# The query normaliser of block 1 of each linear-attention layer spread through sixteen DRAM rows instead of indicator matmuls, with instruction order, engine choice and buffers searched anew

## The chip, the core and the metric

The kernel runs on one core of a Trainium2 chip. The core has five engines with a queue of their own: PE (TensorE, matmuls; PEld is its weight load), DVE (VectorE), ACT (ScalarE), POOL (GpSimd) and SP (SyncE), which here issues the DMAs. An engine takes its instructions in the order in which the program lists them; engines wait for one another through semaphores. The metric is device time in microseconds (us) of one execution, as the median of several runs. The profile comes from one further execution.

## What is computed

Four layers, A B A B, act on x of 2048 tokens by 512 features (bf16), each behind a layer norm and with a residual. There are 32 heads of 16 features. The change lies in layer A, a linear attention whose features are two softmaxes, of sign plus and minus:

```python
phi_q = concat([softmax(pq), softmax(-pq)], -1)      # per head, 32 features
phi_k = concat([softmax(pk), softmax(-pk)], -1)
kv  = einsum("bhsf,bhsd->bhfd", phi_k, v)
z   = einsum("bhsf->bhf", phi_k)
num = einsum("bhqf,bhfd->bhqd", phi_q, kv)
den = einsum("bhqf,bhf->bhq", phi_q, z)[..., None] + 1e-6
x   = x + (num / den) @ wo
```

Layer B is a local attention: each token sees 8 keys, two tokens apart.

## The kernel before, in words

The 2048 tokens are four blocks of 512 (b = 0 to 3); L is 0 or 1, the first or second pair of layers A and B. A weight fold at the start joins the query and key projections with `w_phi`, so that one matmul gives pq or pk. The stages carry the names of their functions and the digits L and b:

- `s_a1` (lines 582 on, stage a1_Lb): key projection `mk`, value projection `mv`, exponentials `ek` of both signs, the sums of 16 by a tree of additions on DVE (`t8` to `t1`), reciprocals as exp(-ln) on ACT (`rr`), the product `mul`, and the sums kv and z over all tokens in PSUM (`kv`).
- `s_a2` (688 on, a2_Lb): query projection `mq` into PSUM, four products of four matmuls per block; `eq` writes the exponentials of both signs to the tile `Eq`, eight ACT instructions per block; `ms` sums them per head by 32 small matmuls, `rs` takes the reciprocal `rS` (an Ln and an Exp on ACT).
- `s_akv` (730 on): once per L, when all four blocks have added to kv: copy of kv to SBUF (`ev`), transposes (`tr`), then the masked matrices `ZM` (`z`) and `R` (`r`) on DVE.
- `s_a3` (770 on, a3_Lb), the stage that the change touches: `md` gives the denominators by 32 small matmuls of `Eq` with `ZM`; `dr` (line 786, two DVE instructions), `ln` (794, Ln and Exp on ACT) and `rho` (798, DVE) give the normaliser rho, one number for each head, sign and token, in a tile of 128 partitions by 256. Each of these numbers must then multiply the 16 feature rows of its head in `Eq`. There are two ways to do this:
  - By indicator matmuls: `bc` (803) spreads one sign of rho over the feature rows with 16 matmuls of 32 by 128 into four PSUM banks; for each of the 4 banks of each of the two signs `bev` (841) either copies the bank to SBUF as bf16 on ACT (tile `bs`) or does nothing, and `mulp` (812) multiplies 128 by 512 of `Eq` on DVE, from `bs` or straight from PSUM.
  - Through DRAM: `wr` (819) writes rho to a scratch tensor `rd` of 16 rows by two DMAs of 64 KB, `rdb` (826) reads it back for one sign, each row for eight partitions, as a tile `Prho` of 512 KB, and `muld` (833) multiplies 128 by 2048 of `Eq` on DVE, two instructions per block.
- `s_a4` (885 on): `mo` applies `R` (32 small matmuls, reading all of `Eq`), `ev` copies to the tile oT, and `s_out` (508) does the output projection `mm`, the residual `res` (on DVE, or on ACT where PE adds x by a matmul with the identity), the squares for the layer norm `sq` (ACT), `var`, `ln`, `nmr`, the layer norm application `ap`, and the transposed copy of the result by DMA or on PE.
- `s_b1` (919 on): query, key and value projections of layer B (`mm`, line 927), values written to DRAM (`vwr`) and read back four times (`vrep`). `s_b2`: the products `prod` of queries with eight shifted keys (DVE, 128 by 4096), their sums on PE (`lgt`), exponentials and their normaliser `pt`. `s_b3`: products `pav` with the values (DVE, 128 by 4096), sums (`mo`) and the output projection.

Which blocks go through DRAM stands in `_OPT["rho_dma"]` (line 39). Nothing is scheduled at run time: `stages` lists the steps as threads, `run` issues them in the order of the string `_ORDER` (line 56), `_CHOICE` (99) says for each step that two engines can do which of them does it, and `_SLOTS` (107) gives every tile its buffer in the pools `big` (8), `med` (16), `t2` (6) and `ps` (8 PSUM banks). On each engine a step stands behind all that were issued to it earlier.

## Time and profile before

| what | value |
|---|---|
| median of 3 runs | 328.9 us (327.68 to 329.29) |
| the profiled execution's own time | 327.1 us |
| its span in the profile | 325.3 us |
| moved by DMA | 41.05 MB, mean 126 GB/s |
| DVE is last busy at | 320.55 us |

The 1.8 us between span and time lie around the profiled span. The profile gives, for each engine, the union of its busy intervals; matmuls overlap in their pipeline, so that a matmul's own duration is longer than the distance from one to the next. A row of the timeline has start, duration, engine, line, operation, tiles and count, and in brackets the idle time of the engine ahead of it with what ended it.

### The profile page before, as it was taken

The numbers are of one execution on the slowest core, as the hardware profiler recorded it, in microseconds if no ns is written. First come the engines' busy times: TensorE is split into PE (matmuls) and PEld (weight loads), VectorE is DVE, ScalarE is ACT, GpSimd is POOL, SyncE is SP. The second block draws the span as 40 slices with busy tenths as digits, with TensorE's granted clock in tenths as the row PEclk, the third lists the DMA queues.
The fourth block names the chain that finished last, engine by engine and source line by source line (L and its number), as shares of the span: only waits on it lengthen the run. The fifth ranks groups of instructions, "written<-read, shape, count | busy, mean of one in ns | idle before, by whom it ended". The sixth has DMA issues, their size and how long they took to land.

```text
span 325.3 us, 8025 instructions
## 1 busy us (share of the span) xinstructions
PE 309.9 (95%) x3174; PEld 150.0 (46%) x3174; DVE 299.5 (92%) x435; ACT 283.2 (87%) x641; POOL 21.6 (7%) x50
## 2 busy tenths in 40 slices
PE   8999999999999999989999999979999999999883
PEld 3654456445454444444444445644544454533331
DVE  5999996988999998999999899699999999999993
ACT  4999989998898899899998999999999998775570
POOL 4000000000001001000000000000023031500000
PEclk9999999999999999999999999999999999999998
DMA  7948100023535897692740300023533947728952
GB/s 201 344 105 209 52 2 4 2 59 90 115 98 131 166 233 230 214 221 45 222 134 1 66 1 2 4 56 93 148 68 121 229 116 185 213 103 246 248 181 91
DMA packets 43853, 41.05 MB, mean 126 GB/s; under 512 B 28448, under 2 KB 37664, under 8 KB 43808
## 3 DMA queue, kind: packets, MB, share of 16 engines
q1 hardware_dynamic: 43280, 40.45, 46.8%
q8 instruction: 26, 0.43, 0.5%
q14 instruction: 19, 0.16, 0.2%
q10 hardware_dynamic: 528, 0.02, 0.1%
HBM read 27.74 MB, written 6.95 MB: 107 GB/s over the span
## 4 chain that ended last, share of the span: by engine, by line
PE 38%; ACT 21%; DVE 20%; DMA 7%; issue 6%; SPq 5%; DVEq 0%; ACTq 0%
PE ps L927 15%; PE ps L519 8%; SPq L983 5%; ACT sqd L539 3%; DMA Vg<-vd 3%; DVE pav L1075 3%; DVE prod L1013 3%; DMA vd<-V 3%; ACT Eq L705 3%; PE ps L697 3%; DVE Ek L650 2%; PE ps L604 2%; DVE stat L492 2%; ACT xn L445 2%; ACT oT L191 2%
## 5 line engine op out<-in xcount | busy, mean ns | idle before, releaser
L927 PE MATMUL ps<-xnT,WB 128*128 128x512 bf16 x384 | 87.2, 380 | 0.1
L1075 DVE TENSOR_TENSOR pav<-PT,Vg 128x4096 bf16<-128x4096 bf16 (+1 forms) x34 | 72.2, 2164 | 1.7 <-DMA Vg<-vd 1.2
L1013 DVE TENSOR_TENSOR prod<-QT,K 128x4096 bf16<-128x4096 bf16 x32 | 71.8, 2284 | 0.3
L927 PEld LDWEIGHTS <-WB 128*128 128x128 bf16 x384 | 42.6, 114 | 42.2 <-issue 5.6
L519 PEld LDWEIGHTS <-oT 128*128 128x128 bf16 x256 | 24.1, 98 | 32.2 <-ACT oT L191 2.7
L705 ACT ACTIVATE Eq<-ps 128x512 bf16<-128x512 f32 x64 | 34.9, 615 | 0.3 <-PE ps L697 0.3
L191 ACT CAST oT<-ps 128x512 bf16<-128x512 f32 (+1 forms) x55 | 30.4, 588 | 5.5 <-PE ps L1084 5.1
L598 ACT ACTIVATE Ek<-ps 128x512 bf16<-128x512 f32 x64 | 34.0, 621 | 0.0
L519 PE MATMUL ps<-WoB,oT 128*128 128x512 bf16 x128 | 32.5, 380 | 0.9 <-ACT oT L191 0.9
L697 PE MATMUL ps<-xnT,WA 128*128 128x512 bf16 x128 | 31.6, 379 | 0.6 <-ACT bs L846 0.3
L539 ACT ACTIVATE sqd<-x 128x512 bf16<-128x512 bf16 x48 | 30.4, 632 | 1.8 <-DVE x L532 0.6
L604 PE MATMUL ps<-WA,xnT 128*128 128x512 bf16 x128 | 30.5, 379 | 0.1
L592 PE MATMUL ps<-WA,xnT 128*128 128x512 bf16 x128 | 30.5, 379 | 0.0
L519 PE MATMUL ps<-WoA,oT 128*128 128x512 bf16 x128 | 29.8, 380 | 0.1
L532 DVE SCALAR_TENSOR_TENSOR x<-ps,x 128x512 bf16<-128x512 f32 x35 | 22.9, 683 | 0.2 <-PE ps L519 0.2
L529 ACT ACTIVATE x<-ps 128x512 bf16<-128x512 f32 x29 | 16.8, 607 | 4.9 <-PE ps L522 4.9
L191 ACT CAST QT<-ps 128x512 bf16<-128x512 f32 x31 | 18.3, 600 | 3.0 <-PE ps L927 3.0
L1084 PE MATMUL ps<-pav,indAV 128*32 128x512 bf16 (+1 forms) x272 | 17.3, 369 | 2.9 <-DVE pav L1075 2.9
L604 PEld LDWEIGHTS <-xnT 128*128 128x128 bf16 x128 | 12.3, 98 | 15.6 <-issue 1.0
L445 ACT ACTIVATE xn<-x,nmr,rstd 128x512 bf16<-128x512 bf16 x23 | 18.1, 819 | 1.4 <-DVE nmr L434 1.3
L191 ACT CAST K<-ps 128x512 bf16<-128x512 f32 x31 | 17.9, 597 | 1.1 <-PE ps L927 1.0
L592 PEld LDWEIGHTS <-xnT 128*128 128x128 bf16 x128 | 12.2, 98 | 14.2 <-issue 0.2
(128 smaller groups left out, 434.9 us busy)
## 6 DMA issues: line engine op xcount, KB each, us to landing
Vg<-vd SPq DMA_DIRECT2D x128, 131.5 KB, 3.4
vd<-V SPq DMA_DIRECT2D x8, 528.0 KB, 3.3
Prho<-rd SPq DMA_DIRECT2D x8, 512.0 KB, 5.7
x<-in_A_x_dram SPq DMA_DIRECT2D x3, 512.0 KB, 7.5
WB<-in_B_wqkv_dram SPq DMA_DIRECT2D x3, 512.0 KB, 9.1
wraw<-in_A_wqkv_dram SPq DMA_DIRECT2D x4, 256.0 KB, 3.9
out_dram<-x SPq DMA_DIRECT2D x8, 128.0 KB, 2.4
out_dram<-x SPq DMA_DIRECT2D x4, 256.0 KB, 2.4
```

The source lines that it names most:

```text
L191: self.nc.scalar.copy(out=out, in_=in_)
L445: nc.scalar.activation(out=xn, in_=xt, func=ACT.Identity, scale=rstd, bias=sh)
L519: nc.tensor.matmul(y[:], lhsT=oT[:, c, t * P:(t + 1) * P], rhs=Wo()[:, c, :], start=(c == 0), stop=(c == NB - 1 and not onpe))
L539: nc.scalar.activation(out=sqd[:], in_=xb[:, t, :], func=ACT.Square, accum_out=T["ss"][:, t:t + 1])
L592: nc.tensor.matmul(pk[:], lhsT=xnT[:, t, k, :], rhs=self.WA[:, k, D:2 * D], start=(k == 0), stop=(k == NB - 1))
L598: nc.scalar.activation(out=T["E"][:, t, s, :], in_=T["k", t][:], func=ACT.Exp, scale=1.0 - 2.0 * s)
L604: nc.tensor.matmul(pv[:], lhsT=xnT[:, t, k, :], rhs=self.WA[:, k, 2 * D:3 * D], start=(k == 0), stop=(k == NB - 1))
L697: nc.tensor.matmul(pq[:], lhsT=self.WA[:, k, hb * P:(hb + 1) * P], rhs=xnT[:, :, k, :], start=(k == 0), stop=(k == NB - 1))
L705: nc.scalar.activation(out=self.Eq[L, b][s][:, :, hb, :], in_=T[hb][:].rearrange("p (t i) -> p t i", t=4), func=ACT.Exp, scale=1.0 - 2.0 * s)
L927: nc.tensor.matmul(pp[:], lhsT=self.WB[:, k, i * D + c:(i + 1) * D:NB], rhs=xnT[:, :, k, :], start=(k == 0), stop=(k == NB - 1))
L1013: nc.vector.tensor_tensor(out=pr[:], in0=QT[:, c:c + 1, :].to_broadcast([P, NW, TB]), in1=win, op=ALU.mult)
L1075: nc.vector.tensor_tensor(out=pv, in0=PT[:, :, lo:lo + n].unsqueeze(1).to_broadcast([P, NB, 2, n]), in1=vw, op=ALU.mult)
```

## The change

`rho_dma` gains the blocks (0, 1) and (1, 1), so that block 0 alone of each layer A keeps the indicator matmuls. `_ORDER`, `_CHOICE` and `_SLOTS` are replaced as wholes; no function is changed.

```diff
 _OPT = {
-    "rho_dma": ((0, 2), (0, 3), (1, 2), (1, 3)),
+    "rho_dma": ((0, 1), (0, 2), (0, 3), (1, 1), (1, 2), (1, 3)),
...
 _ORDER = """
-23 2 8 a d 0 9 b 0 4f j k i i i o j i i i i i 0 t 1m 1n i i l i p 2 1m 1o 0 t o u 3 i i i m n 1t 1u 1m 1p q t 1m
...
+8 4f 30 i 0 j i i i 9 k i i i i i i i 2 1m 0 0 a b i i 2 1m i j l m 0 3 o p t 1n o f t u 1o 1t 1u 1m 1p 3 n 1m
...
 _CHOICE = (
-    "1111110111000111111110000000100001001101000101010111101100001000001101010000100000000000111110111101"
...
+    "0111110011100111111110100000100001000110010100100011101111110100111111001000100001000000101100110101"
...
 _SLOTS = {
-        "0123456789abcdef153437ad3335063b941fced7a94c1f5c09a1f3bcaa45e09673210af7b3c45164425511f457186d32bc0a"
...
+        "0123456789abcdef24536399d4d9b79c831ef268314dfe68bbb714689c0e7182b3f9d2e6307fc1be2cb111901cea418d2b7f"
...
```

In instructions, PE loses 64 weight loads and 64 matmuls of `bc`, SP gains 4 writes and 4 reads, and DVE and ACT change in these kinds (count before, count after):

```
DVE  mulp from bs 128x512     14   3      ACT  bev 128x512          14   3
DVE  mulp from PSUM 128x512   18  13      ACT  copies of v to vaug  21  25
DVE  muld 128x2048             8  12      ACT  ap of the layer norm 23  26
DVE  copies of v to vaug      11   7
DVE  ap of the layer norm     41  38
```

Five further kinds of PSUM copies change by one or two instructions. The order around the kv sum of the second layer A, as the strings give it (digits are L and b, then the step's number; d: straight from PSUM, s: through `bs`):

```
PE  before: kv13(3), mq13(0), tr, ms12, md10, mq13(1), md12, bc10(0), bc10(1), md11, mq13(2), mq13(3), mo10
PE  after:  kv13(3), mq12(3), tr, md10, ms12, md11, md12, bc10(0), ms11, bc10(1), mq13(0) to mq13(3), mo10

ACT before: kv copy, 1 eq12, 2 eq13, rs12, ln10, 2 eq13, bev10, ln12, bev10 x3, eq13, bev10, eq13, ln11, 2 eq13, ...
ACT after:  kv copy, 5 eq12, ln10, rs12, bev10, ln12, rs11, bev10, ln11, 8 eq13, ev10, rs13, ln13, res10, ...

DVE before: z, r, dr10, rho10, dr12, mulp10 d s d, rho12, dr11, mulp10 s s d s s, rho11, ev10 x2, mulp11 d d s s, ...
DVE after:  z, r, dr10, rho10, dr12, rho12, mulp10 d, dr11, mulp10 d s, rho11, mulp10 d d s d d, ev10 x3, dr13, muld12 x2, ...

SP  before: wr12, rdb12 x2, wr13, rdb13 x2
SP  after:  wr12, wr11, rdb12 x2, rdb11 x2, wr13, rdb13 x2
```

From `mo10` to the first product of layer B, `prod10(0)`, ACT has 15 PSUM copies, 9 `sq` and 2 layer norm `ln` before, and 8 copies, 12 `sq` and 3 `ln` after, beside the same 3 `res`, 3 `ap`, one copy of 1024, `rs13` and `ln13`. From `prod10(0)` to the end DVE has 16 `prod`, 16 `pav` and 4 `pt` in both. On PE the projections of layer B that stand ahead of the step `mo13` are seven before (four of keys, two of queries, one of values) or seven after (three of queries and four of keys). In the first layer A, PE has `ms00`, two kv steps, `mq02(0)`, `tr`, `ms01`, `md00`, `md01`, `mq02(1)`, `bc00(0)` before, and `ms00`, `tr`, `md00`, `ms01`, `md01`, `mq03(0)`, `bc00(0)` after.

More of the change, by code (lines that the diff above doesn't have):

```diff
@@ new lines @@
+6x 6t 6v 4w 4z 50 6y 51 4z 50 4z 52 6v 50 53 4v 4z 50 54 81 81 86 88 88 6v 6z 88 9f 9i 84 9f 9j 9n 55 56 55 55
+9k 58 6v 55 6z 70 85 7q 87 7q 9p 73 71 72 74 9p 59 57 57 89 9w 9x 88 5a 57 89 57 5b 57 9w 89 89 8a 9p 9p bh 9q
+9o 9s 8a 9r 87 87 bs 87 89 5b 5f 5d 5e 5c aw 8a at bt bt bs bs 9t bt bt bt bt 9x 9w 9x ax 9w 5g 9x at at au 88
+8b 8b 8b au au au aw 9y ay 9y ai bq br br al am 9x 9y al 87 al 9e 9v 9v 9v aj aj an 8c 8d 8c 8c 8b 8c bq bq 8g
+bq ao 8f 8e 8h 8h at 8h au au br br 8i 8j ai au 9w br br br br au 9z a0 a1 9v 9v 9z a0 9z 9z 8k a0 bq a3 a0 a2
@@ L103 @@
-    "0000000001111011000000000000000000000000000000000010110000000000000000000001111"
+    "0111110011100111111110100000100001000110010100100011101111110100111111001000100001000000101100110101"
+    "0000110100000000000000001111101000100000100000000000000000001000111110000001000100000000000000000000"
+    "1111110000000000010000011011011111011100001010000100000000000111110010000111000000000000000001111010"
+    "000000001000000000000000000000000001110000000000000000000001111"
 )
```

90 lines of the change are left out of this document (41 added, 49 removed).

## Prediction

> **What bounds the kernel now.** First the page's engine shares, then the table of busy time by stage, which says where the shares are full.
>
> ```profile
> PE 309.9 (95%) x3174; PEld 150.0 (46%) x3174; DVE 299.5 (92%) x435; ACT 283.2 (87%) x641; POOL 21.6 (7%) x50
> ```
>
> ```profile
> 6.00:209.20 203.20, 199.77 (x2135) 99.07 (x2136) 189.90 (x297) 190.04 (x431) 5.21 (x17) 1.00 0.44 113
> 209.20:217.90 8.70, 7.16 (x216) 3.98 (x212) 7.19 (x21) 8.37 (x21) 0.00 (x0) 1.00 0.09 19
> 217.90:239.80 21.90, 21.71 (x255) 10.55 (x247) 21.21 (x52) 21.00 (x54) 0.00 (x0) 1.00 0.49 116
> 239.80:290.00 50.20, 50.07 (x364) 24.09 (x363) 49.12 (x33) 44.88 (x101) 12.94 (x9) 1.00 0.58 156
> 290.00:320.55 30.55, 26.43 (x217) 10.03 (x209) 29.60 (x28) 17.51 (x39) 0.00 (x0) 1.00 0.66 198
> ```
>
> The columns of the second view are the stretch and its length, then PE, PEld, DVE and ACT busy. No engine has room to spare over the whole span, but the one that is full changes. Up to 209.20, when DVE starts on the kv sum of the second layer A, PE is idle for 3.4 us of 203.2, DVE and ACT for some 13. From 217.90 to 239.80 DVE and ACT are both within 0.9 us of full. From 239.80, the first product of layer B, to 320.55, when DVE ends, DVE is idle for 2.0 us of 80.75. So the end is: when PE delivers the kv sum, plus the passage to the first product, plus 80.75 us of DVE.
>
> The chain of waits (start, length, what) gives the pace of PE and the pieces that the change moves.
>
> ```profile
> 207.97 0.97 PE ps L697 x4
> 209.16 0.56 PE ps L713 x32
> ...
> 274.91 10.38 PE ps L927 x48
> ```
>
> 48 matmuls of 512 columns in 10.38 us are 216 ns each: PE issues them back to back. A page of the Trainium skill speaks against this reading: "Perfetto Trace Analysis", section "Identifying the Most-Contended Engine", holds matmul busy time for a bad measure and judges TensorE by its weight loads' share. By that rule PE, at 46%, has half its time free and DVE is the bound; this is the fourth rival. The trace goes against it where matmuls stand 216 ns apart with no gap.
>
> **The change part by part.** The work that it takes off stands in the groups by line (count, busy us, mean ns).
>
> ```profile
> L815 DVE TENSOR_TENSOR Eq<-ps,Eq 128x512 bf16<-128x512 f32 x18 | 11.6, 682 | 0.0
> ...
> L835 DVE TENSOR_TENSOR Eq<-Eq,Prho 128x2048 bf16<-128x2048 bf16 x8 | 9.7, 1218 | 0.0
> ...
> L846 ACT CAST bs<-ps 128x512 bf16<-128x512 f32 x14 | 7.9, 600 | 0.1
> ...
> L815 DVE TENSOR_TENSOR Eq<-bs,Eq 128x512 bf16<-128x512 bf16 x14 | 5.5, 417 | 0.0
> ...
> L807 PE MATMUL ps<-rho,indB 32*128 32x128 bf16 x128 | 3.4, 216 | 1.3 <-DVE rho L800 1.3
> ```
>
> DVE: 11 x 0.417 and 5 x 0.682 go, 4 x 1.218 come: -3.1 us. The new choice of engines takes four copies of v and three layer norm applications from it and gives back some three other copies; the nearest rows are the first of these for a copy from PSUM (0.68) and the fourth for 512 columns of bf16 (0.42), which makes -2.7, -1.3 and +2.0: together -5.0 or so. ACT: 11 x 0.600 = -6.6, part of which returns with the moved steps. PE: 64 matmuls; 128 are busy 3.4 us, so -0.9 in each layer. Removed time counts only where its engine is the one that is late. Ahead of 209.20 that is PE, so DVE's and ACT's shares there are costed at nothing: PE's own work covers them, and if it did not, DVE's 5 us would come off (fourth rival). In that stretch PE also reaches the kv sum without one projection of block 3 and without the sums of block 1, which now stand behind it: -0.97 and -0.56 at the rows above. **Term 1: the kv sum is 0.9 + 1.0 + 0.5 = 2.4 us earlier.**
>
> In the first layer A the knot around the kv sum is rearranged too. PE's timeline:
>
> ```profile
> 56.78 0.89 PE L807 MATMUL ps<-rho,indB 32*128 32x128 bf16 x32 [0.74 <-DVE rho L800]
> ```
>
> PE waited 0.74 us for rho. In the new order no projection lies between kv and the transpose, so PE waits there for the copy of kv and for ZM, by the copy and small operations of the second layer (below) 0.6; a projection now covers the wait for rho, and PE then waits about 0.6 for block 0's products, as its second `bc` stands behind four projections. 0.6 + 0.6 - 0.7: **term 2, +0.5 us** (0 to 1.2).
>
> Now the knot of the second layer. DVE's timeline, then ACT's and PE's:
>
> ```profile
> 209.20 0.29 DVE L752 TENSOR_TENSOR ZM<-ps,maskH 128x32 bf16<-128x32 bf16 x2 [1.70 <-PE ps L743]
> ...
> 210.22 0.42 DVE L789 TENSOR_TENSOR s<-ps,rS 128x256 f32<-128x256 f32 x1 [0.40 <-PE ps L781]
> 210.68 0.29 DVE L792 TENSOR_TENSOR Ds<-s 128x128 f32<-128x128 f32 x1
> 211.78 0.42 DVE L800 TENSOR_TENSOR rho<-rS,Ds 128x256 bf16<-128x256 f32 x1 [0.81 <-ACT Ds L796]
> ...
> 212.78 0.68 DVE L815 TENSOR_TENSOR Eq<-ps,Eq 128x512 bf16<-128x512 f32 x1
> ...
> 216.58 0.75 DVE L815 TENSOR_TENSOR Eq<-bs,Eq 128x512 bf16<-128x512 bf16 x2
> ```
>
> ```profile
> 208.49 1.58 ACT L705 ACTIVATE Eq<-ps 128x512 bf16<-128x512 f32 x3
> 209.95 0.41 ACT L719 ACTIVATE rS<-ps 128x256 f32<-128x256 f32 x1
> 210.38 0.42 ACT L720 ACTIVATE rS<-rS 128x256 f32<-128x256 f32 x1
> 211.00 0.40 ACT L795 ACTIVATE Ds<-Ds,deneps_t 128x128 f32<-128x128 f32 x1 [0.20 <-DVE Ds L792]
> 211.44 0.31 ACT L796 ACTIVATE Ds<-Ds 128x128 f32<-128x128 f32 x1
> ...
> 233.24 0.63 ACT L539 ACTIVATE sqd<-x 128x512 bf16<-128x512 bf16 x1
> ...
> 233.99 0.63 ACT L539 ACTIVATE sqd<-x 128x512 bf16<-128x512 bf16 x1
> ...
> 239.17 0.60 ACT L191 CAST QT<-ps 128x512 bf16<-128x512 f32 x1
> ```
>
> ```profile
> 216.71 1.10 PE L900 MATMUL ps<-Eq,R 32*32 32x512 bf16 x32 [0.74 <-DVE Eq L815]
> ```
>
> I count from the start of ZM, 209.20, as zero. Before: rho of block 0 starts at 2.6, its first product at 3.6, its last product ends at 8.1, `mo10` ends at 8.6. After, the kv copy ends at -0.7 as before. ACT then has five exponentials at 0.53 each, to 1.95, and `ln10` of 0.75: rho10 at 2.7, the same. But PE now has the sums of block 2 between `md10` and the other two `md`, and they need the last of those exponentials: they run from 1.95 to 2.5, md11 and md12 follow at 0.56 each, to 3.6, and `dr12` ends at 4.3. On ACT `ln12` stands behind the copy `bev10`, which waits for `bc10(0)` at 4.0, so ACT reaches `ln12` at 4.5 and ends at 5.25; rho12 takes DVE to 5.7. **In the new order DVE waits for rho12 ahead of its first product**, which thus starts at 5.7 and not 3.6. Then eight products, six straight and two through `bs`, at the pace of this timeline 0.6 and 0.35, with `dr11` and rho11: 5.4, so they end at 11.1 and `mo10` at 11.5, 2.9 us later than before. Queued behind rho12 on DVE are all products of block 0, and for these waits `mo10` on PE and from there every copy of oT.
>
> From `mo10` to the first query copy of layer B ACT is full in both. Its list is shorter by 7 copies at 0.49 and longer by 3 `sq` at 0.75 and one layer norm `ln` of two small instructions, for which I take 0.55, under the 0.75 of the Ln and Exp above: -0.6. ACT also idles while the three oT copies and `dr13` run on DVE ahead of `ln13`: +1.1, as `ln13` is ahead of all residual work in its queue. 2.9 - 0.6 + 1.1: **term 3, the first product of layer B is 3.4 us later relative to the kv sum** (bounds: 2.0, if ACT and PE run ahead and take up what DVE loses in block 0, since DVE saves 1.4 in block 1, four products at 0.6 and four at 0.35 against two of 1.2; 4.5, if every copy waits its turn). I take 3.4, as DVE's and ACT's counts agree on it.
>
> The new DMAs: times from SP's timeline and the page's list of issues (last column: us to landing).
>
> ```profile
> 227.08 1.22 SPq L824 DMA_DIRECT2D rd<-rho  x2
> 230.26 1.18 SPq L831 DMA_DIRECT2D Prho<-rd  x2
> ```
>
> ```profile
> Prho<-rd SPq DMA_DIRECT2D x8, 512.0 KB, 5.7
> ```
>
> From rho to the issue of the reads 3.2 us, 5.7 more to landing. In SP's queue wr11 stands ahead of block 2's reads and waits for rho11, at 8.2, so these are issued at 9.5 and 10.1 and land at 15.2 and 15.8. DVE wants them at 14.1 and 15.3; ACT's copies of block 2 follow at about 18.9, which covers the half microsecond. Block 1's reads have six us more. So the transfers cost nothing, unless they are slower (third rival). For a single DMA the Trainium skill, "DMA: Bandwidth & Descriptors", section "Anatomy of one DMA — SWDGE (gpsimd) path", has 2.0 us plus the bytes at 436 GB/s; an estimate by that is 3.2 us for 512 KB, which would leave the third rival no ground. The row's 5.7 decides, and the sum stays as it is.
>
> After the first product DVE has the same list, so its 80.75 us move as they are. PE arrives there with one or two projections of 0.86 fewer done, as the seven of both orders stand behind later residual work; in 239.80 to 290.00 PE is full, so some of this returns as a wait of DVE for its operands: **term 4, +0.4** (0 to 1.7). Other moves of the search, in loads and in the first layer B, I cost at 0, between -2 and +2: PE's 3.4 us of idle time is all that they could win.
>
> Sum: -2.4 + 0.5 + 3.4 + 0.4 = +1.9 us. On the profiled execution's 327.1 that is 329.0; on the median of the runs shown, which lies 1.8 higher, **330.8 us**. Between -2 and +2 for the rest, its own range is 329 to 333.
>
> **The rivals.**
> 1. *It cancels*: the order's lost time is nearer 2 us, and what PE saves pays for it; 328.9, within 1 us. For it: ACT and DVE are both shorter in sum. Against: the list of ACT above has its waits in front.
> 2. *It is faster*: rho12 costs nothing. That decides itself at one place: if the sums of block 2 start by 0.5 after ZM, `ln12` precedes its copy's wait and the first product starts at 4.0. Term 3 is then the 0.4 of rho12 alone, the sum -2.4 + 0.5 + 0.4 + 0.4 = -1.1, and if the search also found 1.3 of PE's idle 3.4 us, -2.4: 326.5. Against it: the exponentials are five at 0.53 in front.
> 3. *The transfers are late*: four reads of 512 KB leave in one burst, where before it was two. From landing to the copies it is a `muld` of 1.2 and 0.6 of `mo12`, so a landing up to 17.1, 7.0 us after the second read's issue, is free. At twice 5.7 it lands at 21.5, 4.4 late, and ACT's queue stands: 335.2. Against it: two reads share the engines already in the 5.7.
> 4. *DVE was the bound all along*: all its 5.0 us come off, 323.9. Against it: its 13 us of idle time ahead of 209.20.
> That the change does not do what it says is excluded by the order of the built program: 64 matmuls fewer, eight DMAs more.
>
> **How the numbers follow.** Forecast 0.42, rival 1 0.24, rival 2 0.18, rival 3 0.11, rival 4 0.05. A measurement of this kernel can tell about 0.5%, 1.6 us, from no change. Slower by more: rival 3 and 0.34 of the forecast, 0.45. Within: rival 1, 0.08 of the forecast and 0.02 of rival 2, 0.34. Faster: 0.16 of rival 2 and rival 4, 0.21. The range 326.0 to 334.8 leaves out rival 4, the lower third of rival 2 and half of rival 3, together 0.17.
>
> **What would show it.** In the profile after: ZM (line 751 there) starts 2 to 3 us earlier than 209.20 (term 1); from it to the first product of line 814 about 5.7 us with rho between them twice, and about 11.5 to the end of `mo10` (term 3); from there some 22 to the first `prod`; DVE idle about 5 us between ZM and `prod`, where it was 2.2. No wait of line 834 for a DMA above 1 us. I am wrong if the first product follows ZM within 4 us, if DVE's stretch after the first `prod` is not 80 to 82 us, or if ZM starts later than before.

## The result and the profile after

The changed kernel takes 329.66 us (median of 20 runs, 328.57 to 330.29); the kernel before takes 327.86 us (median of 20 runs, 326.99 to 330.18). The ratio is 1.0043, 95% interval 1.0028 to 1.0058: 0.43% slower, which lies within the 0.5% that the prediction called no change. The profiled execution takes 328.96 us with a span of 327.2 us; the one of before had 327.1 and 325.3. The prediction's sum for the profiled execution was 329.0. Its forecast of 330.8 for the median is 1.1 us too high.

The page's engine shares, then the busy time by stage, cut at the same events as before's table (ZM, end of `mo10`, first product of layer B, end of DVE):

```profile
PE 306.4 (94%) x3082; PEld 149.0 (46%) x3110; DVE 295.5 (90%) x419; ACT 279.9 (86%) x634; POOL 27.3 (8%) x50
```

```profile
6.00:207.22 201.22, 195.81 (x2046) 98.33 (x2063) 185.03 (x283) 186.13 (x424) 8.12 (x17) 1.00 0.48 120
207.22:218.29 11.07, 8.78 (x253) 5.06 (x257) 8.12 (x20) 10.16 (x24) 0.00 (x0) 1.00 0.17 37
218.29:241.78 23.49, 21.34 (x252) 10.17 (x243) 20.76 (x48) 21.13 (x55) 0.00 (x0) 1.00 0.58 137
241.78:290.00 48.22, 47.42 (x318) 23.41 (x299) 47.72 (x31) 40.53 (x88) 13.81 (x9) 1.00 0.58 157
290.00:322.05 32.05, 28.37 (x240) 10.36 (x241) 30.86 (x28) 19.32 (x42) 1.89 (x1) 1.00 0.69 209
```

By the page PE is busy 3.5 us less than before, DVE 4.0, ACT 3.3, and the kernel is slower all the same. PE's 3.5 is too much: 28 of its matmul records are missing (3082 beside 3110 weight loads). e_rho_later below has the same list on PE and all 3110 records, and shows 308.4 us, 1.5 less than before. The loss stands in the second and third row, from ZM to the first product of layer B. Behind `mo10` alone PE was idle for 0.2 us of 21.9 before, and is now idle for 2.15 of 23.49.

DVE's timeline (start, length, engine, line, operation; in brackets the idle time ahead and what ended it) from ZM to that first product, then ACT's and PE's:

```profile
207.22 0.29 DVE L751 TENSOR_TENSOR ZM<-ps,maskH 128x32 bf16<-128x32 bf16 x2 [1.93 <-PE ps L742]
...
212.00 0.42 DVE L799 TENSOR_TENSOR rho<-rS,Ds 128x256 bf16<-128x256 f32 x1 [0.81 <-ACT Ds L795]
212.35 0.68 DVE L814 TENSOR_TENSOR Eq<-ps,Eq 128x512 bf16<-128x512 f32 x1
...
218.29 1.89 DVE L188 CAST oT<-ps 128x512 bf16<-128x512 f32 x3 [0.60 <-PE ps L899]
...
221.11 1.23 DVE L834 TENSOR_TENSOR Eq<-Eq,Prho 128x2048 bf16<-128x2048 bf16 x1 [0.28 <-DMA Prho<-rd]
223.38 1.23 DVE L834 TENSOR_TENSOR Eq<-Eq,Prho 128x2048 bf16<-128x2048 bf16 x1 [1.04 <-DMA Prho<-rd]
...
241.78 2.29 DVE L1012 TENSOR_TENSOR prod<-QT,K 128x4096 bf16<-128x4096 bf16 x1
```

```profile
220.87 0.40 ACT L794 ACTIVATE Ds<-Ds,deneps_t 128x128 f32<-128x128 f32 x1 [1.19 <-DVE Ds L791]
...
225.50 1.54 ACT L190 CAST oT<-ps 128x512 bf16<-128x512 f32 x3
```

```profile
213.08 3.61 PE L696 MATMUL ps<-xnT,WA 128*128 128x512 bf16 x16 [0.41 <-DVE Eq L814]
...
216.63 0.39 PE L899 MATMUL ps<-Eq,R 32*32 32x512 bf16 x3
217.44 0.73 PE L899 MATMUL ps<-Eq,R 32*32 32x512 bf16 x29 [0.43 <-ACT Eq L704]
...
226.12 3.95 PE L518 MATMUL ps<-WoA,oT 128*128 128x512 bf16 x15 [1.02 <-ACT oT L190]
```

ZM starts at 207.22 (before 209.20), the first product of block 0 follows it by 5.13 us (3.58), DVE's copies of oT behind `mo10` by 11.07 (8.69), the first product of layer B by 34.56 (30.60); from there to DVE's end at 322.05 it is 80.27 us (80.75). So the two profiles differ by -1.98 + 3.96 - 0.48 us, and by 0.4 us behind DVE's end: 1.9 us together.

For the experiments three events are enough, all counted from the start of ZM in the second layer A. **First**: the first product of block 0. **O**: the start of block 2's output projection on PE, which in the changed kernel waits for ACT's copies of block 2's output (the row at 226.12, 18.90 us behind ZM). **P1**: the first product of layer B. "Rest" is P1 to DVE's end. All values are of the profiled execution of each kernel; the ratio is to the kernel before, timed beside it.

| kernel | ZM at | first | O | P1 | rest | ratio (95%) |
|---|---|---|---|---|---|---|
| before | 209.20 | 3.58 | - | 30.60 | 80.75 | 1 |
| after | 207.22 | 5.13 | 18.90 | 34.56 | 80.27 | 1.0043 (1.0028 to 1.0058) |
| splice_a | 208.37 | 4.40 | - | 31.48 | 80.75 | 1.0017 (1.0002 to 1.0033) |
| splice_b | 209.53 | 6.27 | 20.89 | 38.21 | 80.26 | 1.0187 (1.0168 to 1.0206) |
| before_no1 | 209.66 | 3.74 | - | 30.32 | 80.76 | 0.9970 (0.9954 to 0.9986) |
| after_no1 | 208.67 | 5.12 | 18.90 | 34.53 | 80.27 | 1.0058 (1.0036 to 1.0080) |
| e_rho_later | 207.11 | 3.89 | 18.76 | 34.46 | 80.27 | 1.0045 (1.0022 to 1.0067) |
| e_exp_ahead | 207.42 | 5.11 | 19.06 | 34.73 | 80.31 | 1.0049 (1.0017 to 1.0081) |
| e_exp_rho | 207.67 | 3.87 | 18.67 | 34.34 | 80.26 | 1.0038 (1.0011 to 1.0065) |
| e_sq_later | 207.58 | 5.12 | 18.90 | 33.92 | 85.00 | 1.0166 (1.0142 to 1.0190) |
| e_sq_spread | 208.01 | 5.13 | 18.96 | 33.99 | 89.59 | 1.0292 (1.0240 to 1.0343) |
| e_both | 208.45 | 3.89 | 18.70 | 33.71 | 85.02 | 1.0199 (1.0161 to 1.0237) |
| e_best | 207.22 | 3.88 | 19.57 | 34.59 | 87.69 | 1.0270 (1.0214 to 1.0327) |
| e_back | 209.35 | 5.24 | 20.18 | 35.86 | 80.26 | 1.0137 (1.0118 to 1.0156) |
| g_mo | 207.59 | 3.89 | 21.97 | 37.64 | 80.28 | 1.0135 (1.0086 to 1.0184) |
| g_ev | 207.33 | 3.89 | 18.87 | 36.09 | 80.27 | 1.0043 (1.0019 to 1.0068) |
| g_fill | 208.02 | 5.13 | 25.79 | 44.07 | 80.26 | 1.0366 (1.0321 to 1.0411) |
| e_read_first | 207.29 | 5.13 | 18.91 | 36.28 | 80.26 | 1.0089 (1.0071 to 1.0108) |
| h_ot | 208.11 | 5.12 | 18.92 | 36.10 | 80.26 | 1.0129 (1.0101 to 1.0156) |
| h_all | 207.86 | 3.89 | 18.00 | 35.88 | 80.28 | 1.0094 (1.0073 to 1.0115) |

One warning comes with the second column: eleven of these kernels have the instructions of the changed kernel up to ZM, in the same order, and their profiles put ZM between 207.11 and 208.45. Absolute times of one profile are good to about a microsecond; distances behind ZM repeat to 0.1 us where nothing differs.

### The profile page after: what moved, and what is told of

Its sections match the earlier page's. It is cut to its first block, busy times and chain, and to the rows that moved or that the text cites. A ratio compares the mean times of both kernels' runs of the same rounds, so it can differ in the third digit from the quotient of the medians.

```text
span 327.2 us, 7875 instructions
## 1 busy us (share of the span) xinstructions
PE 306.4 (94%) x3082; PEld 149.0 (46%) x3110; DVE 295.5 (90%) x419; ACT 279.9 (86%) x634; POOL 27.3 (8%) x50
## 4 chain that ended last, share of the span: by engine, by line
PE 38%; ACT 24%; DVE 21%; issue 7%; DMA 4%; SPq 3%; DVEq 0%; ACTq 0%
PE ps L926 16%; DVE prod L1012 7%; PE ps L518 7%; ACT Eq L704 6%; ACT sqd L538 4%; DVE pav L1074 4%; ACT Ek L597 3%; DMA Vg<-vd 3%; ACT xn L444 2%; PE ps L603 2%; DVE stat L491 2%; PE ps L1019 2%; PE ps L591 2%; SPq L982 2%; DVE x L531 2%
## 5 line engine op out<-in xcount | busy, mean ns | idle before, releaser
L704 ACT ACTIVATE Eq<-ps 128x512 bf16<-128x512 f32 x64 | 34.2, 626 | 0.0
L518 PE MATMUL ps<-WoB,oT 128*128 128x512 bf16 x121 | 31.7, 380 | 0.4
L190 ACT CAST oT<-ps 128x512 bf16<-128x512 f32 (+1 forms) x53 | 28.3, 587 | 3.4 <-PE ps L1083 3.3
L696 PE MATMUL ps<-xnT,WA 128*128 128x512 bf16 x128 | 30.6, 380 | 0.4 <-DVE Eq L814 0.4
L603 PE MATMUL ps<-WA,xnT 128*128 128x512 bf16 x124 | 30.2, 379 | 0.3
L591 PE MATMUL ps<-WA,xnT 128*128 128x512 bf16 x123 | 29.7, 379 | 0.3 <-issue 0.2
L444 ACT ACTIVATE xn<-x,nmr,rstd 128x512 bf16<-128x512 bf16 x26 | 20.2, 819 | 2.0 <-DVE nmr L433 1.9
L190 ACT CAST K<-ps 128x512 bf16<-128x512 f32 x30 | 16.9, 598 | 5.1 <-PE ps L926 5.1
L603 PEld LDWEIGHTS <-xnT 128*128 128x128 bf16 x128 | 12.5, 98 | 15.3 <-issue 0.7
L649 DVE TENSOR_TENSOR Ek<-Ek,rk 128x4096 bf16<-128x4096 bf16 (+1 forms) x10 | 18.6, 1860 | 0.6 <-ACT rk L644 0.6
```

What stands on the lines that cost most here:

```text
L190: self.nc.scalar.copy(out=out, in_=in_)
L518: nc.tensor.matmul(y[:], lhsT=oT[:, c, t * P:(t + 1) * P], rhs=Wo()[:, c, :], start=(c == 0), stop=(c == NB - 1 and not onpe))
L591: nc.tensor.matmul(pk[:], lhsT=xnT[:, t, k, :], rhs=self.WA[:, k, D:2 * D], start=(k == 0), stop=(k == NB - 1))
L603: nc.tensor.matmul(pv[:], lhsT=xnT[:, t, k, :], rhs=self.WA[:, k, 2 * D:3 * D], start=(k == 0), stop=(k == NB - 1))
L696: nc.tensor.matmul(pq[:], lhsT=self.WA[:, k, hb * P:(hb + 1) * P], rhs=xnT[:, :, k, :], start=(k == 0), stop=(k == NB - 1))
L704: nc.scalar.activation(out=self.Eq[L, b][s][:, :, hb, :], in_=T[hb][:].rearrange("p (t i) -> p t i", t=4), func=ACT.Exp, scale=1.0 - 2.0 * s)
```

## The experiments

### The removed work, the new path and the order apart

*before_no1* is the kernel before without any spreading and multiplying for block 1; *after_no1* is the changed kernel without it. Both then leave block 1's queries unnormalised. They do the same work and differ only in order, choice of engines and buffers.

```diff
 before_no1, s_a3 for b == 1
-bc(s): 16 matmuls; bev(s, t): copy; mulp(s, t): product
+nothing
 after_no1, s_a3 for b == 1
-wr(): 2 DMAs; rdb(s): 1 DMA; muld(s): product
+nothing
```

> Leaves out the spreading of block 1's rho and the multiplication of its queries by it in both layers A (its queries stay unnormalised); order, engines and buffers as before. It shows what that work is worth in the order of before. Theory: 0.9 us of PE in the first layer, and in the second a passage from ZM to the first product of layer B that is 1 to 3 us shorter, as DVE loses 4.1 us of products between 219 and 223 but ACT keeps its list: ratio 0.988 to 0.994. Rival 'DVE was the bound': 0.975 or less. Rival 'hidden anyway': 0.997 or more.

> The same work left out of the changed kernel (write, reads and multiplication of block 1's rho in both layers A); its own order, engines and buffers stay. Both this kernel and before_no1 then compute the same, and only the order differs. Theory (order, not transfers): ZM 2 us ahead of before's, rho12 still ahead of the first product, which follows ZM by 5.1 us, mo10 ends 11 us after ZM, and the loss against before_no1 stays: ratio to before 0.993 to 1.003, above before_no1 by 0.4% or more. Rival 3 (transfers late): the waits for block 2's rows, 0.28 and 1.04 us, go, and the kernel falls to before_no1's time or below.

Measured: 0.9970 and 1.0058. All the work that the change could take away is worth 0.3% in the order of before. In the order of after no cost of the new path is seen: without it the ratio is 1.0058, with it 1.0043, and the intervals overlap. Order, engines and buffers together, 1.0058 against 0.9970, make 0.9%; no run tells the three apart. DVE's timeline of before_no1, then of after_no1:

```profile
209.66 0.29 DVE L752 TENSOR_TENSOR ZM<-ps,maskH 128x32 bf16<-128x32 bf16 x2 [1.70 <-PE ps L743]
...
223.45 1.23 DVE L841 TENSOR_TENSOR Eq<-Eq,Prho 128x2048 bf16<-128x2048 bf16 x1 [3.64 <-DMA Prho<-rd]
...
239.98 4.53 DVE L1019 TENSOR_TENSOR prod<-QT,K 128x4096 bf16<-128x4096 bf16 x2
```

```profile
208.67 0.29 DVE L751 TENSOR_TENSOR ZM<-ps,maskH 128x32 bf16<-128x32 bf16 x2 [1.93 <-PE ps L742]
...
224.17 1.23 DVE L841 TENSOR_TENSOR Eq<-Eq,Prho 128x2048 bf16<-128x2048 bf16 x1 [0.34 <-DMA Prho<-rd]
```

In before_no1 the passage is 30.32 us long although DVE has lost 4 us of products in it. They were hidden nearly in full, as the expectation's last rival says; the row at 223.45 shows behind what. Without the products DVE reaches block 2's first rows early and waits 3.64 us for them, 13.8 us behind ZM; in before it came to them 13.85 us behind ZM without a wait. So nearly all that DVE saved in this layer went into one wait for a DMA: 0.3% is what the work is worth in this order, not what a faster DVE could gain in another. In after_no1 the second rows of block 2 keep DVE waiting for 0.34 us instead of 1.04, with block 1's write and reads out of the queue, and P1 stays at 34.53. Rival 3 of the prediction, late transfers, does not carry the loss.

### Halves of the two orders

*splice_a* follows the changed kernel up to the second kv sum, and the kernel before from there; *splice_b* the other way round.

```diff
 splice_a
-order of before, steps up to akv1; block 1 of the first layer by matmuls
+order of after, the same steps;   block 1 of the first layer through rows
 splice_b
-order of before from akv1 on; block 1 of the second layer by matmuls
+order of after, the same steps; block 1 of the second layer through rows
```

> The order of the changed kernel up to the second layer's kv sum (block 1 of the first layer A through DRAM rows), then the order of the kernel before (block 1 of the second layer by matmuls). Theory (terms 1 and 3 of the prediction): only the 0.9 us of the first layer's matmuls leave, and the first product of layer B again follows ZM by 30.6 us; ratio to before about 0.997 (0.995 to 0.999). Rival 'the DRAM path itself costs' (block 1's rows arrive late, in the first layer too): 1.000 or more. Rival 'the order of the second layer is innocent': the ratio of the changed kernel, about 1.004.

> The order of the kernel before up to the second layer's kv sum, then that of the changed kernel (block 1 of the second layer through DRAM rows, of the first by matmuls). Theory: the 1.0 and 0.5 us of work that moved behind the kv sum bring ZM 1.5 us earlier, the 0.9 of the first layer stay, and the passage from ZM to the first product of layer B takes 34.6 us as in the changed kernel instead of 30.6: ratio about 1.007 (1.005 to 1.010). Rival 'the first layer carries the loss': at most 1.002, with splice_a above 1.002.

Measured: 1.0017 and 1.0187. Both theories fail. DVE's timeline of splice_a:

```profile
208.37 0.29 DVE L752 TENSOR_TENSOR ZM<-ps,maskH 128x32 bf16<-128x32 bf16 x2 [3.46 <-PE ps L743]
...
210.19 0.42 DVE L789 TENSOR_TENSOR s<-ps,rS 128x256 f32<-128x256 f32 x1 [1.21 <-PE ps L781]
...
239.85 4.53 DVE L1013 TENSOR_TENSOR prod<-QT,K 128x4096 bf16<-128x4096 bf16 x2
```

ZM is 0.83 us ahead of before, as expected, but DVE then waits 1.21 us for the denominators (0.40 in before), and P1 comes at 239.85, where it was at 239.80. What is gained ahead of ZM is not gained at P1: PE's projections and sums stand behind the kv sum instead of ahead of it. PE's timeline of splice_b:

```profile
206.20 2.22 PE L667 MATMUL ps<-Ek,vaug 128*33 128x64 bf16 x128
209.10 0.40 PE L743 MATMUL ps<-ident,kvT 128*128 128x128 bf16 x4 [0.68 <-ACT kvT L191]
...
211.62 1.94 PE L781 MATMUL ps<-Eq,ZM 128*32 128x128 bf16 x64
```

Here 1.5 us of PE work went from ahead of ZM, and ZM did not come earlier (209.53, before 209.20). The sums of block 1, 0.56 us, stood ahead of the kv sum. They came back as waits: ahead of the kv sum PE waits 1.3 us in all for DVE's products with the values (`pav`), where it waited 0.6. The projection, 0.97 us, stood between the kv sum and the transposes, where PE has to wait for ACT's copy of kv in any case, and now does so for 0.68 us: from the end of the sum to ZM it is 1.11 us, in before 1.23. Term 1 priced PE as the only engine that sets ZM, and here DVE and ACT stand beside it. In the changed kernel DVE's list ahead of ZM is shorter too, 185.0 us busy for 189.9; that this is why ZM comes earlier there is likely, but no run shows it. The last row shows a second surprise, 64 small matmuls in 1.94 us that take 1.08 in the changed kernel; it is taken up at the end, and it makes splice_b slower for a reason that is not the order's alone.

### The reason given in term 3

*e_rho_later* undoes what the prediction called the cause.

```diff
 DVE, second layer A
-dr10 rho10 dr12 rho12 mulp10(0,0) dr11 ...
+dr10 rho10 dr12 mulp10(0,0) rho12 dr11 ...
```

> The changed kernel with rho of block 2 and its write moved behind the first product of block 0 in DVE's order, nothing else. Theory of the prediction's term 3 ('DVE waits for rho12 ahead of its first product'): the product of 0.68 us fits into the wait of 0.81 us, so the first product follows ZM by about 4.0 us instead of 5.1, mo10 ends 0.7 us earlier, and the ratio to before falls from about 1.004 to about 1.002. Rival (ACT sets the passage: in the changed kernel it is busy 31.3 of the 34.6 us from ZM to the first product of layer B): the first product is 1 us earlier but ACT's exponentials of block 3 and its copies start within 0.3 us of where they were, and P1, the first product of layer B, moves by 0 to 0.3 us: ratio unchanged.

Measured: 1.0045, the changed kernel's ratio. DVE's and PE's timelines:

```profile
211.00 0.68 DVE L814 TENSOR_TENSOR Eq<-ps,Eq 128x512 bf16<-128x512 f32 x1
```

```profile
217.12 0.74 PE L899 MATMUL ps<-Eq,R 32*32 32x512 bf16 x29 [0.58 <-ACT Eq L704]
...
225.87 3.96 PE L518 MATMUL ps<-WoA,oT 128*128 128x512 bf16 x16 [0.78 <-ACT oT L190]
```

The first product is 1.24 us nearer to ZM, just as computed. But rho12 and `dr11` behind it then wait for ACT (0.21 and 0.29 us), so that DVE's last product of block 0 ends only 0.2 us earlier (10.26 us behind ZM for 10.46); `mo10` waits 0.58 us for an exponential of block 3, O moves by 0.14 us and P1 by 0.10. The wait was real, and taking it away alone gains next to nothing.

Why should `mo10`, which reads block 0 alone, wait for block 3? The program gives its four outputs the PSUM buffers ps0 to ps3, and ps3 is the one that `mq13(2)` filled and that the exponentials of block 3 still read. In the changed kernel's rows at 216.63 and 217.44 PE breaks off after three of the 32 matmuls, at the first that writes ps3. In the kernel before `mo10` has other buffers (ps7, ps0, ps1, ps2) and waits for DVE's product instead. So the choice of buffers is a rival of the order here; no run changes it alone, and it stays untested.

### ACT's list

The rival became the next theory, and was tried from two sides: ACT's exponentials (*e_exp_ahead*, and with the move above *e_exp_rho*), and the squares of block 2 ahead of P1 (*e_sq_later*, *e_both*, *e_sq_spread*, *e_best*).

```diff
 e_exp_ahead, ACT
-vaug, 1 eq12, kv copy, 5 eq12, ln10
+vaug, 3 eq12, kv copy, 3 eq12, ln10
 e_sq_later
-4 sq12, 4 sq11, var12, ln12, nmr12, ... prod10(0), prod10(1)
+4 sq11, ... prod10(0), 4 sq12, var12, ln12, nmr12, prod10(1)
 e_sq_spread
+squares among the copies of layer B, var12, ln12, ap12 behind prod11(0)
```

> The changed kernel with two of the five exponentials of block 2 put ahead of the copy of kv in ACT's queue, nothing else; ACT stands idle for 1.02 us there, waiting for the kv sum. Theory (ACT's queue sets the passage from ZM to P1, the first product of layer B): ZM moves by at most 0.2 us, ACT has 1.06 us less behind it, mo10 ends and P1 comes 0.7 to 1.0 us earlier relative to ZM: ratio to before about 1.002. Rival (DVE, through rho or the rows, sets it): rho of block 0 is 0.3 us earlier at most and P1 stays where it was, 34.5 us behind ZM: ratio about 1.004.

> The moves of e_exp_ahead and e_rho_later together in the changed kernel: with ACT relieved, DVE's wait for rho of block 2 may count after all. If it does, P1 comes 1.5 us earlier relative to ZM, ratio about 1.000; if not, the result is that of e_exp_ahead.

> The changed kernel with the four squares of block 2, their variance, root, offset and one application of the layer norm moved behind the first product of layer B, nothing else (before had two of these squares ahead of it and two behind). Theory (ACT's list sets the passage, and block 2's residual work, which the new path puts ahead of block 1, lengthens it): ACT loses 4 x 0.75 us and two small instructions ahead of its query copies, the first product follows ZM by about 32.5 us instead of 34.6, and as ACT has room in layer B the time falls by 1 to 2 us: ratio to before 0.998 to 1.002. Rival (PE or the residual adds on DVE set it): under 0.5 us, ratio unchanged.

> Both moves of e_rho_later and e_sq_later in the changed kernel. If DVE's wait for rho and ACT's list each carry a part, the ratio is lower than either alone, by the sum of the two: 0.995 to 1.000. If ACT's list alone sets the passage, the ratio is that of e_sq_later within 0.002.

> The changed kernel with block 2's four squares moved among the copies of layer B, behind the first product, and its variance, layer norm and transpose behind that layer's first four products, so that DVE does not stand for ACT's squares as it did in e_sq_later (3.44 us). Theory: the first product of layer B again follows ZM by 33.9 us instead of 34.6, the rest of the kernel stays at 80.3 us, ratio 0.002 below the changed kernel's. Rival (the squares must be there that early, since layer B wants block 2's normalised input): the rest grows by more than 0.7 us and the ratio is that of the changed kernel or above.

> The moves of e_exp_ahead, e_rho_later and e_sq_spread together in the changed kernel. If ACT's queue sets the passage, they add up: mo10 ends 1.5 us and P1 comes 1.5 to 2.5 us earlier relative to ZM, ratio 0.996 to 1.000. If another engine sets it, the ratio is 1.002 or above.

Measured: 1.0049 and 1.0038 for the first two. In e_exp_ahead ACT gives up its 1.02 us of idle time ahead of the kv copy and waits 0.84 us for `dr10` instead, which cannot come before ZM; P1 is at 34.73. ACT's row:

```profile
209.13 0.40 ACT L794 ACTIVATE Ds<-Ds,deneps_t 128x128 f32<-128x128 f32 x1 [0.84 <-DVE Ds L791]
```

The squares did bring P1 from 34.56 to 33.92 us, but the rest grew from 80.27 to 85.00. DVE's timeline of e_sq_later:

```profile
241.50 2.28 DVE L1012 TENSOR_TENSOR prod<-QT,K 128x4096 bf16<-128x4096 bf16 x1
...
247.29 0.16 DVE L550 TENSOR_TENSOR q<-q,ss 128x4 f32<-128x4 f32 x1 [3.44 <-ACT sqd L538]
...
248.14 4.49 DVE L1012 TENSOR_TENSOR prod<-QT,K 128x4096 bf16<-128x4096 bf16 x2
```

DVE's second product stands behind the variance, and that behind ACT's squares: 3.44 us, and layer B begins with one product instead of three. Spread further back, the squares hold up layer B more (rest 89.59), and e_both and e_best only add that to the others. These four misplace a step that layer B needs; they say that block 2's squares are worth 0.6 us at P1, and that they are not to be had later at that price.

### Work put back, moved or split around mo10

> The changed kernel with the sums of block 1 and their root (32 matmuls, 0.56 us on PE; two instructions, 0.78 us on ACT) put back ahead of the transpose of kv. It tests the second half of term 1. By the prediction's term 1 this makes ZM 0.5 us later, and the passage from ZM to the first product of layer B shorter only by what it removes there. Theory (PE sets what is ahead of ZM): ZM 0.5 us later relative to the end of the kv sum, passage 0.3 to 0.8 shorter as ACT and PE have less in it: ratio within 0.001 of the changed kernel's. Rival (moving work behind the kv sum was a real gain): ratio higher by 0.0015 or more.

> e_rho_later with the last two projections of block 3 and their four exponentials put behind mo10 and its first copy (before has one and a half of them there). Theory A (block 3's work stands in the way of block 0's chain): mo10, which waits 0.58 us for an exponential in e_rho_later, ends 0.5 us earlier, at about 9.7 us behind ZM, and the first product of layer B comes 0.5 to 1 us earlier than 34.5. Theory B (a chain of waits between the engines that has no other work to fill it): PE's 1.8 us of projections only move behind mo10, and the first product stays within 0.3 us of 34.5 or comes later. Ratio 1.002 by A, 1.004 or more by B.

> e_rho_later with one of DVE's three copies of block 0's output given to ACT, which stands idle for 1.19 us there (two and two, as in the kernel before). Theory A (the split of the copies delays the output projection): PE's wait of 0.45 us for DVE's copies shrinks, ACT's wait goes, and the first product of layer B comes 0.4 to 0.7 us earlier: ratio about 1.003. Theory B: less than 0.3 us, ratio about 1.0045 as e_rho_later.

> The changed kernel with the matmul path of block 1 put back in the second layer A, behind mo10: 32 matmuls (0.9 us of PE), eight copies (four on ACT), eight products (4 us of DVE) come, two multiplications of 1.2 us, a write and two reads go. Theory B (the removed path filled waits that stay without it): the work goes into the waits, and the first product of layer B comes at most 0.5 us later than 34.6 behind ZM, or earlier: ratio 1.002 to 1.006. Rival (DVE or PE is full there): it comes 1.5 to 2.5 us later, ratio 1.009 or more.

```diff
 e_back, ACT                           g_mo, PE
-kv copy, 5 eq12, ln10, rs12, ..., rs11  -bc10(1), mq13(0) to mq13(3), mo10
+rs11, kv copy, 5 eq12, ln10, rs12, ...  +bc10(1), mq13(0), mq13(1), mo10, mq13(2), mq13(3)
 g_ev                                  g_fill, block 1 of the second layer
-ev10: 3 copies DVE, 1 ACT              -wr11, rdb11 x2, muld11 x2
+ev10: 2 copies DVE, 2 ACT              +bc11, bev11, mulp11 behind mo10
```

e_back also puts the sums `ms11` back ahead of the transposes on PE; g_mo and g_ev have the move of e_rho_later as well.

Measured: 1.0137, 1.0135, 1.0043 and 1.0366. In e_back the two instructions for block 1's root stand ahead of the kv copy on ACT and wait there for PE, so the kv copy and ZM come late, which was not meant: it shows the price of that slip and not of term 1. In g_mo PE waits 1.74 us ahead of `mo10`, and 0.84 more in it for DVE's last product, so that `mo10` ends 10.7 us behind ZM as in e_rho_later: the gain that theory A expects there is out. P1 at 37.64 says less about it: on ACT the copy of block 0's output still stands behind all exponentials of block 3, and now waits for the projections that went behind `mo10` (2.91 and 0.62 us). g_ev is the changed kernel's time: the split of the copies is not the cause either. In g_fill PE stands 3.20 us behind an addition on ACT and DVE 3.15 us behind ACT's root of block 3: the copies and products that were put back stand ahead of work of the other blocks that all engines wait for. Besides, its granted clock is at a half from 229 to 240 us, which is taken up at the end. So it does not test what it was made for; whether the old path could fill these waits from another place stays open.

### The waits that the trace names

*e_read_first* takes DVE's wait for block 2's rows, *h_ot* PE's wait for ACT's copies of block 2's output, *h_all* both and the wait for rho.

```diff
 e_read_first, SP
-wr12, wr11, rdb12 x2, rdb11 x2
+wr12, rdb12 x2, wr11, rdb11 x2
 h_ot, ACT
-res10, sq10, res10, sq10, res10, sq10, 3 ev12, sq10
+res10, sq10, res10, res10, 3 ev12, sq10, sq10, sq10
```

> The changed kernel with the two reads of block 2's rows put ahead of the write of block 1's rho in SP's queue, nothing else. Rival 3 (transfers late): the rows arrive 1 us or more earlier, DVE's waits of 0.28 and 1.04 us go, and the first product of layer B comes 0.5 to 1.3 us earlier: ratio 1.000 to 1.003. The prediction's cover (ACT's copies of block 2 come later anyway): the waits go but the first product stays within 0.2 us of 34.5 behind ZM, ratio 1.004.

> The changed kernel with two squares of block 0 put behind ACT's three copies of block 2's output, for which PE stands 1.02 us. If this wait is what lengthens PE's list, the first product of layer B comes 0.8 to 1.0 us earlier (ratio 1.001 to 1.002). If block 0's chain through ACT (squares, layer norm, transposes, query projection) sets it, PE waits later for the layer norm instead and the first product comes 0 to 1 us later: ratio 1.004 to 1.007.

> The changed kernel with the moves of e_rho_later, e_read_first and h_ot. If the waits named by the trace are the cause, the first product of layer B follows ZM by 31.5 to 32.5 us and the ratio is 0.996 to 0.999. If they only follow from a chain that has no other work beside it, they reappear elsewhere, the passage stays above 33.5 us and the ratio at 1.003 or more.

Measured: 1.0089, 1.0129 and 1.0094; each relief made it slower. SP's queue in the changed kernel and in e_read_first (issues, by start and length), then DVE's row of the latter:

```profile
212.46 3.72 SPq L823 DMA_DIRECT2D rd<-rho  x4
216.35 2.53 SPq L830 DMA_DIRECT2D Prho<-rd  x4
```

```profile
212.53 1.26 SPq L823 DMA_DIRECT2D rd<-rho  x2
216.27 1.21 SPq L830 DMA_DIRECT2D Prho<-rd  x2
217.57 1.22 SPq L823 DMA_DIRECT2D rd<-rho  x2
223.43 1.18 SPq L830 DMA_DIRECT2D Prho<-rd  x2
```

```profile
228.07 1.22 DVE L834 TENSOR_TENSOR Eq<-Eq,Prho 128x2048 bf16<-128x2048 bf16 x1 [2.03 <-DMA Prho<-rd]
```

The reads of block 2 leave at 216.27, where they left at 216.35: what they wait for is the landing of their own write, 3.7 us behind its issue, and block 1's write stood in that gap for nothing. Put behind the reads, block 1's write is issued at 217.57, its reads leave at 223.43 and not about 217.6, and DVE waits 2.03 us for them: 3.8 of the 5.8 us were covered. The prediction gave block 1's rows six us of room.

In h_ot P1 went from 34.56 to 36.10 us behind ZM, and O stayed at 18.92. ACT's row, then DVE's and PE's:

```profile
226.39 1.56 ACT L190 CAST oT<-ps 128x512 bf16<-128x512 f32 x3 [1.41 <-PE ps L899]
```

```profile
230.12 0.16 DVE L550 TENSOR_TENSOR q<-q,ss 128x4 f32<-128x4 f32 x1 [1.59 <-ACT sqd L538]
```

```profile
227.03 3.10 PE L518 MATMUL ps<-WoA,oT 128*128 128x512 bf16 x12 [0.77 <-ACT oT L190]
230.94 1.02 PE L518 MATMUL ps<-WoA,oT 128*128 128x512 bf16 x4 [0.81 <-DVE x L531]
```

The copies did not come earlier. ACT is free for them 1.4 us sooner, but they start 18.28 us behind ZM in both kernels: in the changed kernel ACT comes to them without idle time, in h_ot it stands for `mo12`, which stands for DVE's product with block 2's second rows, 1.07 us late here. ACT's list and these rows thus end at nearly the same time, and relieving one of the two does not move O. What is left of h_ot is its price: the variance of block 0 now waits 1.59 us for the squares; DVE's additions behind it come late, and PE waits for them 0.81 us. P1 moves by 1.54 us, the length of two squares with their small reads (0.76 us each in ACT's timeline). That is a one-to-one answer: block 0's squares on ACT have no slack here. In h_all O comes at 18.00, and the waits are back behind it, 1.53 us and 0.35 us on PE.

## Why the prediction was right and wrong

**Terms 1 and 2, ZM earlier by 1.9 us**: 1.98 in the profiles. By the spread of ZM among like kernels it is 0.8 to 2.1 us, so the close hit says little. The reason, PE alone, was too simple: splice_b took 1.5 us of PE's work away and gained nothing.

**Term 3, the passage longer by 3.4 us**: 3.96. First product 5.13 us behind ZM (forecast 5.7), copies behind `mo10` at 11.07 (11.5), ACT's copies of block 2 at 18.28 (18.9), ACT's wait ahead of `ln13` 1.19 (1.1), DVE's idle time in the passage 5.7 (about 5). The size holds within its bounds; its stated cause does not. The step "In the new order DVE waits for rho12 ahead of its first product" is true, and taking the wait away is worth 0.1 us at P1. What the runs show in its place is a regularity. In after, after_no1, e_rho_later, e_exp_ahead and e_exp_rho, P1 follows O by 15.63 to 15.70 us, and O lies between 18.67 and 19.06; in e_back and g_mo, where O lies at 20.18 and 21.97, it is 15.68 and 15.67. So the loss is made ahead of O, and comes through to P1 one to one. In before the like row on PE, with the last quarter of block 0's output projection and block 1's (224.19, 14.99 us behind ZM), lies 15.61 us ahead of P1. Ahead of O PE waits for ACT, whose queue holds block 0's additions and squares ahead of block 2's copies: after_no1 has block 2's second rows 0.7 us earlier and O where it was. But the rows are close behind, as h_ot shows. Behind O PE runs without a pause to the last projection that P1 needs. It does not set the 15.7 us alone: in the four kernels that take block 2's squares out of this stretch they are 15.01 to 15.03 with the same list on PE, so the last 0.65 us belong to these squares and the variance behind them. That ACT's queue, and not the buffers or a step further ahead, is what makes O late is read from the waits; no run brought O back to where it would give P1 at 30.6. In before PE's list for this passage is 28.88 us of 30.60, in after 30.12 of 34.56: 1.2 us of work more and 2.7 us of idle time more. The projection and the sums that stood ahead of ZM, less the 0.9 of matmuls, are 0.6 of the 1.2; what the rest is was not looked into.

**Term 4, +0.4 us behind P1**: the rest is 0.48 us shorter, and 0.4 comes back behind DVE's end. The term had the wrong sign; no run asks why.

**The sum** of 329.0 for the profiled execution met 328.96, and that is luck. Term 3 was 0.6 us too small and term 4 0.9 too large, the 0.4 behind DVE's end were not foreseen, and these cancel; nor does one profile place ZM better than to a microsecond.

**Transfers**: the second rows of block 2 come 1.04 us late for DVE, a little over the limit that the prediction set, and it costs nothing at P1 (after_no1), as ACT's copies are the later ones, if only just (h_ot). Rival 3 is out. Rival 4, DVE as the bound, is out: before_no1 takes 8.1 us of DVE's busy time away (291.4 for 299.5) and gains 0.3%, with 3.64 us of it turned into a wait for rows. Rival 2 had the first product at 4.0 us and 326.5 us for the kernel; e_rho_later has it at 3.89 and the changed kernel's time. Rival 1, that it cancels, is half right: gains ahead of ZM and losses behind it, with 0.4% left over.

**The steps that failed** are two. In the mechanism it is the path of term 3: "Queued behind rho12 on DVE are all products of block 0, and for these waits `mo10` on PE and from there every copy of oT". With rho12 put behind the first product (e_rho_later) that product came 1.24 us earlier, and P1 0.10 us. In its place the runs show that the loss stands ahead of O, where PE waits for ACT's copies of block 2, and that P1 follows O by 15.7 us whatever DVE's first products do; that ACT's order alone makes O late is not shown. In the number it is the last line of the sum, "on the median of the runs shown, which lies 1.8 higher, **330.8 us**". The median of three runs, 328.9, was carried along as the base; with 20 runs it is 327.86, so 1.0 of the 1.1 us by which the forecast is too high comes from the base. Seen from the right base 330.8 is a loss of 2.9 us, and 1.8 were measured.

The class does not hang on the base. The medians differ by 1.8 us (forecast 1.9, which is 0.58% of 327.86), but the ratio of the runs, 0.43%, lies under the 0.5% that was called no change. With a spread of 327.0 to 330.2 in single runs a sum of +0.6% was too near to that border to be called slower.

What stays open: whether any order with the rows for block 1 has the short passage of before, and what part the buffers have in the long one. Thirteen rearrangements of this one did not reach it. In the order of before, before_no1 says, no more than 0.3% would be won.

## What to carry to other kernels

Measure what the work to be removed is worth by leaving it out in the old order, before its removal is priced engine by engine: here 16 products on DVE (8.1 us of its busy time), six copies on ACT (2.1) and 64 matmuls on PE (2.0) were worth 0.3% together. Then look what the freed engine waits for instead. Where three engines are each over 85% busy, follow one chain from event to event and not the waits one by one; in these runs a wait that was removed came back at the next engine. Take the base of a small difference from as many runs as the difference needs.

## What the hardware did that was not expected

In some of these kernels the granted clock falls in the middle of the work, although PE is never idle for long. PE's timeline of e_back, then the stretches (columns: PE, PEld, DVE, ACT and POOL busy, then the granted clock) of e_back and of the changed kernel:

```profile
208.91 0.40 PE L742 MATMUL ps<-ident,kvT 128*128 128x128 bf16 x4 [1.41 <-ACT kvT L190]
...
215.33 5.20 PE L696 MATMUL ps<-xnT,WA 128*128 128x512 bf16 x16 [1.34 <-DVE Eq L814]
```

```profile
206.00:210.00 4.00, 2.30 (x70) 1.30 (x71) 0.62 (x3) 2.42 (x6) 0.00 (x0) 1.00 0.00 0
210.00:214.00 4.00, 2.92 (x144) 2.15 (x133) 1.86 (x5) 3.61 (x10) 0.00 (x0) 1.00 0.02 4
214.00:218.00 4.00, 2.67 (x7) 0.99 (x8) 3.72 (x9) 2.17 (x6) 0.00 (x0) 0.64 0.19 37
```

```profile
206.00:210.00 4.00, 3.27 (x132) 2.34 (x136) 1.61 (x6) 3.90 (x10) 0.00 (x0) 1.00 0.02 4
210.00:214.00 4.00, 2.84 (x89) 1.69 (x78) 2.83 (x8) 3.19 (x8) 0.00 (x0) 1.00 0.07 14
214.00:218.00 4.00, 3.57 (x45) 1.38 (x43) 3.69 (x8) 3.97 (x10) 0.00 (x0) 1.00 0.32 62
```

The 16 projections take 5.20 us, where the changed kernel's row at 213.08 has 3.61. The clock is 0.64 in the mean from 214 to 218; cut into single microseconds it reads 0.58, 0.50, 0.50 and 0.72 from 215 on and 1.00 on either side, which is a half for about 3.4 us. splice_b (from 211) and the profiled execution of g_ev (from 227) show the same half for the same 3.4 us. No single wait in e_back is longer than 1.41 us. The Trainium skill, "TensorE: Matmul & The Clock Gate", section "Part 1: The HAM clock gate (the "warmup" mystery)", ties the half clock to an idle window of about 3.4 us, and has one kernel in which frequent short idle times between groups of matmuls were enough. The rows agree with the half clock and with the short idle times; a whole idle window of 3.4 us is not in them.

What opens and shuts it stays open, and the busy share does not divide the cases. In the four microseconds ahead of the fall PE was busy for 2.20 us in e_back, 2.55 in splice_b and 2.41 in g_ev; but h_all was busy for 2.17 of the four from 229, and e_exp_ahead for 2.34 of the four from 209, and in both the clock stayed at 1.00.

One fall adds about 1.6 us to the 16 projections of e_back. Others stand in splice_b (64 matmuls in 1.94 us, and again from 231), g_mo (from 219) and g_fill (from 229 to 240), which is a part of why these four came out worse than their expectations; the mean clock of all their runs is lower too (e_back 0.987 to 0.992, changed kernel 0.994 to 1.000). In g_ev it is in the profiled execution (16 matmuls in 5.54 us), whose P1 in the table is 1.6 us late by it, while the ratio of its runs is the one expected. It can make a part of the spread between runs as well: of the 17 runs of before that were timed beside g_mo the four longest have the four lowest mean clocks (0.990 to 0.993). Among the changed kernel's 20 runs no such relation is seen.
